# Spectral mixer behind linear attention: pinning filler products in the last four modes, and waiting per PSUM bank instead of per pair of banks

## The chip, the cores and the metric

One core of one Trainium2 chip. The metric is the device time of one execution in microseconds (us). The profiled span, from the first to the last instruction, is about 1.8 us shorter than the timed execution.

## The reference

```python
# linear attention with phi = elu + 1, on q, k, v of shape (8, 8, 576, 64)
q_p, k_p = phi(q), phi(k)
kv  = einsum('bhsd,bhse->...', k_p, v)                  # per head 64 x 64
x   = (q_p @ kv) / (q_p @ sum(k_p) + 1e-6)              # -> (8, 576, 512)
# spectral mix: 64 complex modes, each with its own 512 x 512 complex matrix
X   = rfft(x, axis=1)
Y[:, :64] = X[:, :64] @ (w_r + 1j * w_i)                # mode by mode
u   = x + irfft(Y, n=576)
out = u + relu(u @ w_ch)                                # float32
```

(The first einsum is shortened.) The two weight arrays hold 64 x 512 x 512 float32 each, 134 MB together; everything else is small beside them.

## The kernel before

While the weights stream in, one mode per 4.9 us, TensorE multiplies each mode and computes in the gaps what doesn't depend on the spectrum. What is left for after the last weight is the tail: the last rows of the spectrum through `w_ch`, then 36 output tiles of 128 x 512, taken two at a time ("pairs", 18 of them). A pair owns two banks of PSUM, the memory into which TensorE writes its products; here a bank holds one tile of 128 x 512 float32. Each bank is filled with the channel product of x (`channels`), the inverse transform of the spectrum's channel product is added and rectified in place by ScalarE (`rectified`), then the inverse transform itself is added by TensorE, and VectorE adds x and the tile is stored (`finish`).

```python
def keep_warm(n):                      # filler products, result never read
    for _ in range(n):
        nc.tensor.matmul(last_ps[0], id16, wch16[:, 0, :])

def mode_product(kk, ...):
    for t, w in ((1, wr), (0, wi)):
        ...  nc.tensor.matmul(P..., xt_cols(dc, t, kk), w[...], ...)
        if t == 1 and kk >= NM - 4:
            keep_warm(6)
    ...      # copy P to ys, four matmuls ys -> yt
    if NM - 4 <= kk < NM - 1:
        keep_warm(6)
# [cut]
def channels(n):                       # pair n: one tile, two banks
    accs[n] = pool.tile([128, 2, D], F32, tag="acc", bufs=2, ...)
    for i, t in enumerate(pairs[n]):
        ...  pin(nc.tensor.matmul(accs[n][:, i, cols], id16, src, ...))

def rectified(n):
    for i, t in enumerate(pairs[n]):
        add_inverse(accs[n][:, i], t, 1, ...)
    for i in range(2):
        a = accs[n][:, i]
        pin(nc.scalar.activation(out=a, in_=a, func=AF.Relu))

def finish(n):
    ...      # add_inverse(acc[:, i], t, 0) for both banks, then
    pin(nc.vector.tensor_tensor(out=x, in0=acc, in1=x, op=ALU.add))
    store(t0, 2)                       # the first and the last pair: bank by bank
# [cut]
rectified(0); rectified(1); channels(2); finish(0); channels(3); finish(1)
rectified(2); rectified(3); finish(2)
for n in range(4, len(pairs)):
    channels(n); rectified(n); finish(n - 1)
finish(len(pairs) - 1)
```

`pin` keeps an instruction in program order on its engine; what is not pinned the scheduler may move. Waits between engines follow from which instruction touches which tile, and the two banks of a pair are one tile.

Of the kernel before, what the change touches and what calls it, by code (L numbers as in the profile page):

```python
# [13 lines left out]
AF = mybir.ActivationFunctionType  # L14
ALU = mybir.AluOpType
# [32 lines left out]
def kernel(  # L48
# [10 lines left out]
    nc = tc.nc  # L59

    B, H, S, Dh = q.shape
    D = H * Dh
    NM = moe_w_r.shape[0]
    NHP = H // 2
    NDC = D // 128
    NJJ = 4
# [16 lines left out]
    id16 = const.tile([128, 128], F16, name="id16")  # L83
    fwd_sb = const.tile([128, 5, 2 * NM], F16, name="fwd_sb")
    pick_sb = const.tile([128, 16], F16, name="pick_sb")
    wch16 = const.tile([128, NDC, D], F16, name="wch16")
# [10 lines left out]
    def xt_cols(dc: int, t: int, kk: int):  # L97

        c0 = dc * XDC + t * B * NM + kk
        return xt_c[:, c0 : c0 + 31 * NM + 1 : NM]  # L100
# [27 lines left out]
    pin = tc.keep_in_program_order  # L128
# [196 lines left out]
    def w_get(kk: int):  # L325
        if kk not in w_in:
            w_in[kk] = [w_load(kk, half, wpool, "w", W_KEEP) for half in range(2)]
        return w_in.pop(kk)

    def keep_warm(n: int):  # L330

        for _ in range(n):
            nc.tensor.matmul(last_ps[0], id16, wch16[:, 0, :])

    def mode_product(kk: int, ps, stage, yt_ps):

        wr, wi = w_get(kk)
        st = stage.tile([128, D], F16, tag="ystage", bufs=2, name=f"ys{kk}")

        n_part = 2 if kk == NM - 1 else 1  # L340
        pw = D // n_part
        P = [
            ps.tile([128, D], F32, tag="P", bufs=2, name=f"P{kk}_{i}")[:, 0:pw] for i in range(n_part)
        ]
        for t, w in ((1, wr), (0, wi)):
            for i in range(n_part):
                for dc in range(NDC):
                    nc.tensor.matmul(  # L348
                        P[i][dc * 32 : dc * 32 + 32, :], xt_cols(dc, t, kk),
                        w[:, dc, i * pw : i * pw + pw],  # L350
                        start=(t == 1), stop=(t == 0), tile_position=(0, dc * 32),
                    )
            if t == 1 and kk >= NM - 4:
                keep_warm(6)
        for i in range(n_part):
            dst = st[:, i * pw : i * pw + pw]
            if (kk + i) % 2 == 0:
                nc.vector.tensor_copy(out=dst, in_=P[i])  # L358
            else:
                nc.scalar.copy(out=dst, in_=P[i])  # L360
        for ec in range(NDC):
            nc.tensor.matmul(  # L362
                yt_ps[:, ec, kk % 8, :], st[:, ec * 128 : ec * 128 + 128], pick_sb
            )
        if NM - 4 <= kk < NM - 1:
            keep_warm(6)

    while pending:
        w_next()
# [20 lines left out]
    def mode(kk: int):  # L390
        nonlocal yt_ps
        if kk % 8 == 0:
            yt_ps = psW.tile([128, NDC, 8, 2 * B], F32, tag="yt", bufs=1, name=f"yt{kk // 8}")
        mode_product(kk, psW, ystage, yt_ps)
        if kk == NM - 2:
            nc.vector.tensor_copy(out=YT[:, :, NE : NM - 1, :], in_=yt_ps[:, :, 0 : NL - 1, :])
        elif kk == NM - 1:
            nc.vector.tensor_copy(out=YT[:, :, NM - 1, :], in_=yt_ps[:, :, NL - 1, :])
        elif kk % 8 == 7:
            nc.vector.tensor_copy(out=YT[:, :, kk - 7 : kk + 1, :], in_=yt_ps)  # L400
# [13 lines left out]
    def x_of(t: int):  # L414
        if t < B * NJJ:
            return x_main[t // NJJ][:, t % NJJ, :]
        i = t - B * NJJ
        return x_tail[i // 2][:, i % 2, :]

    def e0_parts(t: int):  # L420

        if t < B * NJJ:
            b, jj = divmod(t, NJJ)
            return [(slice(0, D), E0[b][:, jj * D : jj * D + D])]
        i = t - B * NJJ
        hw = D // 2
        return [(slice(h * hw, h * hw + hw), E0[2 * i + h][:, NJJ * D : QW]) for h in range(2)]
# [4 lines left out]
    last_ps = []  # L432
# [64 lines left out]
    last = sW.tile([128, 2, D], F16, tag="last", bufs=1, name="last")  # L497
    EARLY, LATE, BOTH = 1, 2, 3

    def add_inverse(acc, t: int, half: int, what: int = BOTH):  # L500

        mm = lambda o, l, r: pin(
            nc.tensor.matmul(o, l, r, start=False, stop=True, skip_group_check=True)  # L503
        )
        if t < B * NJJ:
            parts = [(t // NJJ, slice(0, 128), slice(t % NJJ * 128, t % NJJ * 128 + 128))]
        else:
            i = t - B * NJJ
            parts = [(2 * i + h, slice(h * 64, h * 64 + 64), slice(512, 576)) for h in range(2)]
        for b, r, sel in parts:  # L510
            if what == BOTH:
                mm(acc[r, :], inv_sb[:, sel], YZ[b][:, half, :])
                continue
            if what & EARLY:
                mm(acc[r, :], inv_sb[: 2 * NE, sel], YZ[b][: 2 * NE, half, :])
            if what & LATE:
                mm(acc[r, :], inv0_sb[:, sel], last[:, half, :])
# [6 lines left out]
            pairs.insert(len(pairs) - 1, (B * NJJ + 2 * k, B * NJJ + 2 * k + 1))  # L524
    N_PRE = 2
    acc_pools: list = []
    accs: dict[int, object] = {}

    def channels(n: int):
        pool = acc_pools[n % 4 // 2]  # L530
        accs[n] = pool.tile([128, 2, D], F32, tag="acc", bufs=2, name=f"acc{n}")
        for i, t in enumerate(pairs[n]):
            for cols, src in e0_parts(t):
                pin(
                    nc.tensor.matmul(  # L535
                        accs[n][:, i, cols], id16, src, start=(cols.start == 0), stop=False,
                        skip_group_check=True,
                    )
                )

    def rectified(n: int):
        for i, t in enumerate(pairs[n]):
            add_inverse(accs[n][:, i], t, 1, LATE if n < N_PRE else BOTH)
        for i in range(2):
            a = accs[n][:, i]
            pin(nc.scalar.activation(out=a, in_=a, func=AF.Relu))  # L546

    def store(t: int, n_t: int):
        if t < B * NJJ:
            b, jj = divmod(t, NJJ)  # L550
            nc.sync.dma_start(
                out=out[b, 0:512, :].rearrange("(r j) d -> r j d", j=NJJ)[:, jj : jj + n_t, :],
                in_=x_main[b][:, jj : jj + n_t, :],
            )
            return
        i = t - B * NJJ
        for hf in range(2):
            (nc.sync, nc.gpsimd)[hf].dma_start(
                out=out[2 * i + hf : 2 * i + 4 : 2, 512:S, :].rearrange("b r d -> r b d"),
                in_=x_tail[i // 2][hf * 64 : hf * 64 + 64, :, :],  # L560
            )

    def finish(n: int):
        acc = accs.pop(n)
        single = n in (0, len(pairs) - 1)
        t0 = pairs[n][0]
        for i, t in enumerate(pairs[n]):
            if n < N_PRE:
                add_inverse(acc[:, i], t, 0, EARLY)
                add_inverse(acc[:, i], t, 0, LATE)  # L570
            else:
                add_inverse(acc[:, i], t, 0)
            if single:
                x = x_of(t)
                pin(nc.vector.tensor_tensor(out=x, in0=acc[:, i], in1=x, op=ALU.add))  # L575
                store(t, 1)
        if single:
            return
        x = x_main[t0 // NJJ][:, t0 % NJJ : t0 % NJJ + 2, :] if t0 < B * NJJ else x_tail[(t0 - B * NJJ) // 2]
        pin(nc.vector.tensor_tensor(out=x, in0=acc, in1=x, op=ALU.add))  # L580
        store(t0, 2)

    done = 0
# [2 lines left out]
    for kk in range(n_early, NM):  # L586
        mode(kk)
        want = min(len(tiles), (kk - n_early + 1) * len(tiles) // n_spread)
        while done < want:
            channel_product(tiles[done])  # L590
            done += 1
        if kk >= NE - 1:
            while rows_done < min(B, 2 * (kk - NE + 2)):
                form_rows(rows_done)
                rows_done += 1
        if kk == NM - 5:
            psB.release()
            acc_pools.append(
                tc.alloc_tile_pool(name="psT0", bufs=1, space=PSUM, side="right", reuse_waits="tile")
            )  # L600
            for n in range(N_PRE):
                channels(n)
                for i, t in enumerate(pairs[n]):
                    add_inverse(accs[n][:, i], t, 1, EARLY)
            last_ps.append(psW.tile([128, D], F32, tag="zl", bufs=1, name="zl0"))


# [4 lines left out]
    for h in range(2):  # L612
        cols = slice(h * hw, h * hw + hw)
        for ec in range(NDC):
# [3 lines left out]
                    start=(ec == 0), stop=(ec == NDC - 1),  # L618
# [15 lines left out]
    )  # L634

    rectified(0)
    rectified(1)
    channels(2)
    finish(0)
    channels(3)  # L640
    finish(1)
    rectified(2)
    rectified(3)
    finish(2)
# [36 lines left out]
```

## Time and profile before

Median 436.77 us (436.39 to 436.78, 3 runs). What matters:

| part of the span (435.0 us) | from – to, us | what ends last |
|---|---|---|
| stream of weights | to 393.9 | DMA |
| last rows, first two pairs | 393.9 – 403.7 | TensorE at half clock, waits between engines |
| pairs in a steady loop | 403.7 – 425.8 | loop of TensorE and ScalarE, 1.37 us a pair |
| last adds, stores, end | 425.8 – 435.0 | VectorE, stores |

From part 4 of the profile's page of before, the chain of waits by engine:

```profile
DMA 67%; PE 16%; DVE 8%; issue 5%; ACT 2%; POOL 1%; POOLq 0%; DVEq 0%; ACTq 0%
```

From part 2 of the same page: granted TensorE clock in tenths, DMA busy share in tenths, and GB/s, in 40 slices of 10.9 us:

```profile
PEclk9996666675559998657667858586665569966998
DMA  8999999999999999999999999999999999991697
GB/s 149 207 207 209 210 209 209 212 214 219 219 211 213 214 214 213 214 213 214 214 212 214 212 215 213 214 214 213 214 214 213 214 213 214 213 204 34 278 329 265
```

DMA is full until slice 35 (slices are counted from 0). GB/s counts what lands in the core: the weights are float32 in memory and bf16 in the core, so a full DMA shows 213 GB/s here. The clock is low in much of the stream, where DMA sets the pace, and it is down again in slices 35 and 36, just where the stream ends. The view of one source line, the fillers (count; min/median/max ns; first and last start in us):

```profile
L333 PE MATMUL zl<-wch,id x42: 376/379/634, 129.8 to 166.3; 128*128 128x512 f16 x42
```

None of the 42 fillers runs where it was wanted, in the last four modes (377 to 394 us): unpinned, all were moved to 130 to 166 us. The table by stretch of before follows; columns are the stretch, its length, busy us and count of TensorE, its weight loads, VectorE, ScalarE, GpSimd, then granted clock, DMA share and GB/s:

```profile
381.00:386.00 5.00, 1.95 (x16) 0.81 (x16) 0.00 (x0) 0.59 (x1) 0.00 (x0) 0.70 1.06 213
386.00:391.00 5.00, 1.62 (x12) 0.56 (x12) 0.90 (x2) 0.00 (x0) 0.00 (x0) 0.50 1.00 200
...
395.50:397.90 2.40, 2.17 (x12) 1.55 (x12) 0.42 (x2) 0.37 (x1) 0.00 (x0) 0.50 0.00 0
397.90:400.20 2.30, 2.12 (x8) 0.75 (x7) 0.18 (x1) 1.48 (x3) 1.24 (x3) 0.54 0.08 24
400.20:403.70 3.50, 2.65 (x12) 1.04 (x11) 1.38 (x2) 1.34 (x3) 1.66 (x4) 1.00 0.40 134
```

TensorE works 1.6 to 2.0 of 5 us, and the clock goes to 0.50; it is back at 1.00 only after 400.2. Lines of the timeline of before (start, us, engine, line, operation, count, and in brackets the idle time before it with what ended it):

```profile
393.90 0.69 PE L348 MATMUL P<-wi,xt_c 128*32 128x256 bf16 x8 [1.77 <-DMA wi<-in_moe_w_i_dram]
...
395.73 1.89 PE L616 MATMUL zl<-wch,YT 128*128 128x256 f16 x8 [0.32 <-DVE YT L398]
...
398.23 1.87 PE L503 MATMUL acc<-last,inv_sb 128*128 128x512 f16 x4 [0.18 <-DVE last L624]
...
401.22 0.69 DVE L575 TENSOR_TENSOR x_main<-acc,x_main 128x512 f32<-128x512 f32 x1 [3.14 <-PE acc L503]
...
401.97 0.38 PE L503 MATMUL acc<-YZ,inv_sb 112*128 112x512 f16 x1 [0.85 <-DVE x_main L575]
...
403.70 1.02 PE L503 MATMUL acc<-YZ,inv_sb 128*128 128x512 f16 x4
...
417.56 1.17 PE L503 MATMUL acc<-YZ,inv_sb 128*128 128x512 f16 x4
...
418.77 2.52 DVE L580 TENSOR_TENSOR x_main<-acc,x_main 128x1024 f32<-128x1024 f32 x2 [0.22 <-PE acc L503]
...
421.50 2.52 DVE L580 TENSOR_TENSOR x_main<-acc,x_main 128x1024 f32<-128x1024 f32 x2 [0.22 <-PE acc L503]
...
427.69 0.38 PE L503 MATMUL acc<-YZ,inv_sb 128*128 128x512 f16 x1 [0.88 <-DVE x_main L575]
...
428.11 0.69 DVE L575 TENSOR_TENSOR x_main<-acc,x_main 128x512 f32<-128x512 f32 x1 [0.47 <-PE acc L503]
```

Lines 393.9 to 398.2 are the serial end of the spectrum. 401.97 and 427.69 show the price of a pair being one tile: TensorE's product for the second bank waits 0.85 and 0.88 us for VectorE's add of the *first* bank. The adds at 418.77 and 421.50 show the steady loop, two pairs in 2.73 us. The four products at 417.56 take 1.17 us, as every second such group of the loop does. The stores in that time:

```profile
DMA to landing us min/median/max: 2.5/4.6/5.5
```

### The profile page before, as it was taken

How to read it: one execution, taken by the hardware profiler on the slowest of the kernel's cores; microseconds unless marked ns; L12 is line 12 of the kernel's file. 1: busy time of each engine (PE TensorE's matmuls, PEld its weight loads, DVE VectorE, ACT ScalarE, POOL GpSimd, SP SyncE). 2: the span in 40 equal slices, each digit the busy share in tenths (PEclk: the TensorE clock that was granted, in tenths of full speed). 3: DMA queues.
4: the chain of work that ended last, by engine and by line, in shares of the span. 5: the costliest groups of instructions: out<-in, count | busy, mean ns of one | idle time of the engine just before them, and what ended most of it. 6: DMA issues, size and time to landing. Idle time of an engine off the chain costs nothing.

```text
span 435.0 us, 6218 instructions
## 1 busy us (share of the span) xinstructions
PE 291.6 (67%) x2542; PEld 153.5 (35%) x2542; DVE 177.2 (41%) x334; ACT 149.4 (34%) x228; POOL 92.5 (21%) x166
## 2 busy tenths in 40 slices
PE   0358877795039786776775676667587779736992
PEld 0346665562015332222222223222233238413340
DVE  1699998963004242223222323322232222211793
ACT  3687666621002222222222222222222223103681
POOL 4232332122122221222121212122112121102000
PEclk9996666675559998657667858586665569966998
DMA  8999999999999999999999999999999999991697
GB/s 149 207 207 209 210 209 209 212 214 219 219 211 213 214 214 213 214 213 214 214 212 214 212 215 213 214 214 213 214 214 213 214 213 214 213 204 34 278 329 265
DMA packets 35563, 92.38 MB, mean 212 GB/s; under 512 B 3152, under 2 KB 16336, under 8 KB 35536
## 3 DMA queue, kind: packets, MB, share of 16 engines
q0 software_dynamic: 32016, 82.52, 97.5%
q1 hardware_dynamic: 3520, 9.47, 5.8%
q8 instruction: 20, 0.33, 0.3%
q14 instruction: 7, 0.06, 0.0%
HBM read 164.07 MB, written 9.44 MB: 399 GB/s over the span
## 4 chain that ended last, share of the span: by engine, by line
DMA 67%; PE 16%; DVE 8%; issue 5%; ACT 2%; POOL 1%; POOLq 0%; DVEq 0%; ACTq 0%
DMA wr<-in_moe_w_r_dram 34%; DMA wi<-in_moe_w_i_dram 25%; DMA k<-in_k_dram 7%; PE acc L503 4%; PE P L348 3%; DVE x L265 3%; PE eps L462 2%; PE z L485 2%; PE acc L535 2%; PE yp L489 1%; DVE qe L195 1%; DVE q L189 1%; DVE k L189 1%; DVE rd L262 1%; DVE ke L195 1%
## 5 line engine op out<-in xcount | busy, mean ns | idle before, releaser
L114 POOL DMA_DIRECT2D wr<-in_moe_w_r_dram x64 | 34.1, 533 | 136.0 <-PE P L348 112.5
L348 PE MATMUL P<-wi,xt_c 128*32 128x512 bf16 (+1 forms) x260 | 40.7, 525 | 32.0 <-DMA wi<-in_moe_w_i_dram 31.9
L348 PE MATMUL P<-wr,xt_c 128*32 128x512 bf16 (+1 forms) x260 | 42.4, 539 | 27.0 <-DMA wr<-in_moe_w_r_dram 25.7
L470 ACT CAST E<-eps 128x512 f16<-128x512 f32 (+1 forms) x40 | 21.4, 544 | 113.8 <-PE eps L462 113.8
L462 PE MATMUL eps<-wch,xTw 128*128 128x512 f16 x144 | 57.7, 545 | 2.5 <-DVE xTw L459 2.3
L114 POOL DMA_DIRECT2D wi<-in_moe_w_i_dram x64 | 34.1, 534 | 102.9 <-PE P L348 73.9
L447 DVE TENSOR_TENSOR x_main<-nw,rd 128x256 f32<-128x256 f32 x64 | 24.2, 420 | 67.2 <-PE nw L146 67.1
L348 PEld LDWEIGHTS <-xt_c 128*32 128x32 bf16 x520 | 25.8, 161 | 71.7 <-issue 42.4
L358 DVE CAST ys<-P 128x512 f16<-128x512 f32 (+1 forms) x33 | 22.5, 682 | 67.3 <-PE P L348 67.2
L360 ACT CAST ys<-P 128x512 f16<-128x512 f32 (+1 forms) x32 | 18.5, 580 | 78.0 <-PE P L348 77.4
L146 PEld LDWEIGHTS <-qT 64*128 64x128 f16 (+1 forms) x640 | 20.3, 123 | 52.3 <-issue 37.5
L362 PE MATMUL yt<-pick_sb,ys 128*128 128x16 f16 x256 | 16.9, 175 | 32.4 <-DMA pick_sb<-row_pick 21.0
L459 DVE COPY xTw<-xTp 128x512 f16<-128x512 f16 x36 | 15.2, 423 | 46.2 <-PE xTp L457 46.1
L362 PEld LDWEIGHTS <-ys 128*128 128x128 f16 x256 | 12.5, 102 | 46.7 <-issue 23.7
L146 PE MATMUL num<-kv,qT 64*128 64x65 f16 (+1 forms) x320 | 13.1, 218 | 21.2 <-ACT kv L242 17.5
L462 PEld LDWEIGHTS <-xTw 128*128 128x128 f16 x144 | 14.3, 119 | 32.0 <-issue 20.9
L182 ACT ACTIVATE qe<-q 128x1152 f16<-128x1152 f16 x16 | 17.8, 1157 | 22.1 <-DMA q<-in_q_dram 22.1
L211 PE MATMUL qTp<-id,qe 128*128 128x128 f16 x144 | 16.8, 312 | 12.3 <-DVE qe L195 11.9
L454 ACT CAST x16w<-x_main 128x512 f16<-128x512 f32 x32 | 19.9, 621 | 13.3 <-DVE x_main L447 12.8
L546 ACT ACTIVATE acc<-acc 128x512 f32<-128x512 f32 x36 | 20.8, 582 | 6.9 <-PE acc L503 6.0
L503 PE MATMUL acc<-YZ,inv_sb 128*128 128x512 f16 (+2 forms) x80 | 20.5, 381 | 3.3 <-DVE x_main L575 1.7
L265 DVE TENSOR_TENSOR x<-num,rd 128x512 f16<-128x512 f32 x32 | 22.1, 692 | 1.1
(65 smaller groups left out, 382.6 us busy)
## 6 DMA issues: line engine op xcount, KB each, us to landing
wr<-in_moe_w_r_dram POOLq DMA_DIRECT2D x64, 512.0 KB, 18.6
wi<-in_moe_w_i_dram POOLq DMA_DIRECT2D x64, 512.0 KB, 18.7
out_dram<-x_main SPq DMA_DIRECT2D x14, 512.0 KB, 4.6
q<-in_q_dram POOLq DMA_DIRECT2D x8, 576.0 KB, 13.1
k<-in_k_dram POOLq DMA_DIRECT2D x8, 576.0 KB, 14.4
v<-in_v_dram POOLq DMA_DIRECT2D x8, 576.0 KB, 16.5
out_dram<-x_main SPq DMA_DIRECT2D x4, 256.0 KB, 3.7
wch<-in_moe_w_ch_dram POOLq DMA_DIRECT2D x1, 512.0 KB, 20.4
```

What stands on the lines that cost most here:

```text
L114: nc.gpsimd.dma_start(out=w, in_=src[kk].rearrange("(p dc) e -> p dc e", dc=NDC))
L146: mm = nc.tensor.matmul(num[hpo][orow, c0 : c0 + 65], qT[rows, hpp, h2, cols], kv_sb[rows, hpp, h2, :])
L265: nc.vector.tensor_tensor(out=dst.rearrange("p (o c d) -> p o c d", o=2, c=4), in0=nv[:, :, :, 0:64], in1=rden.unsqueeze(3).broadcast_to([ ...
L348: nc.tensor.matmul(P[i][dc * 32 : dc * 32 + 32, :], xt_cols(dc, t, kk), w[:, dc, i * pw : i * pw + pw], start=(t == 1), stop=(t == 0), til ...
L358: nc.vector.tensor_copy(out=dst, in_=P[i])
L362: nc.tensor.matmul(yt_ps[:, ec, kk % 8, :], st[:, ec * 128 : ec * 128 + 128], pick_sb)
L447: nc.vector.tensor_tensor(out=x[orow, o * 256 : o * 256 + 256].rearrange("p (c d) -> p c d", c=4), in0=nv[o][:, :, 0:64], in1=rd_all[b][or ...
L454: nc.scalar.copy(out=x16, in_=x)
L462: nc.tensor.matmul(e_ps, xT[:, c, :], wch16[:, c, :], start=(c == 0), stop=(c == NDC - 1))
L470: nc.scalar.copy(out=dst, in_=e_ps[:, cols])
L503: nc.tensor.matmul(o, l, r, start=False, stop=True, skip_group_check=True)
L546: pin(nc.scalar.activation(out=a, in_=a, func=AF.Relu))
```

## The change

Two independent ideas. First, the fillers and the last four modes are pinned, so that fillers run between the late weights and keep TensorE's clock up. (Twelve a mode as before, but three of them now stand ahead of the `ys` products, to cover the copy.) Second, every instruction on a pair tells which banks it uses, and it is declared independent of instructions on the other bank. The order on each engine in the tail stays the same; only waits go.

```diff
     def keep_warm(n: int):
         for _ in range(n):
-            nc.tensor.matmul(last_ps[0], id16, wch16[:, 0, :])
+            pin(nc.tensor.matmul(last_ps[0], id16, wch16[:, 0, :]))
# [cut: products of modes NM-4 and later are pinned in the same way]
+        if NM - 4 <= kk < NM - 1:
+            keep_warm(3)                 # ahead of the ys products
# [cut]
         if NM - 4 <= kk < NM - 1:
-            keep_warm(6)
+            keep_warm(3)
# [cut]
+    users: dict[int, list] = {}
+    def on_bank(n: int, banks: set, ins):
+        pin(ins)
+        for other, theirs in users.setdefault(n, []):
+            if not banks & theirs:
+                tc.declare_no_dep(ins.ins, other.ins, reason="the other bank of the pair")
+        users[n].append((ins, banks))
# [cut: in channels, add_inverse, rectified and finish pin(...) becomes
#  on_bank(n, {i}, ...); the add over a whole pair is on_bank(n, {0, 1}, ...)]
```

More of the change, by code (lines that the diff above doesn't have):

```diff
@@ L347, in mode_product @@
                 for dc in range(NDC):
-                    nc.tensor.matmul(
+                    mm = nc.tensor.matmul(
                         P[i][dc * 32 : dc * 32 + 32, :], xt_cols(dc, t, kk),
@@ L352, in mode_product @@
                     )
+                    if kk >= NM - 4:
+                        pin(mm)
             if t == 1 and kk >= NM - 4:
                 keep_warm(6)
+        if NM - 4 <= kk < NM - 1:
+            keep_warm(3)
         for i in range(n_part):
@@ L361, in mode_product @@
         for ec in range(NDC):
-            nc.tensor.matmul(
+            mm = nc.tensor.matmul(
                 yt_ps[:, ec, kk % 8, :], st[:, ec * 128 : ec * 128 + 128], pick_sb
             )
+            if kk >= NM - 4:
+                pin(mm)
         if NM - 4 <= kk < NM - 1:
-            keep_warm(6)
+            keep_warm(3)
     while pending:
@@ L498, with add_inverse @@
     EARLY, LATE, BOTH = 1, 2, 3
-    def add_inverse(acc, t: int, half: int, what: int = BOTH):
-        mm = lambda o, l, r: pin(
-            nc.tensor.matmul(o, l, r, start=False, stop=True, skip_group_check=True)
+    def add_inverse(n: int, i: int, t: int, half: int, what: int = BOTH):
+        acc = accs[n][:, i]
+        mm = lambda o, l, r: on_bank(
+            n, {i}, nc.tensor.matmul(o, l, r, start=False, stop=True, skip_group_check=True)
         )
@@ L507, in add_inverse @@
         else:
-            i = t - B * NJJ
-            parts = [(2 * i + h, slice(h * 64, h * 64 + 64), slice(512, 576)) for h in range(2)]
+            p = t - B * NJJ
+            parts = [(2 * p + h, slice(h * 64, h * 64 + 64), slice(512, 576)) for h in range(2)]
         for b, r, sel in parts:
@@ L533, in channels @@
             for cols, src in e0_parts(t):
-                pin(
+                on_bank(
+                    n, {i},
                     nc.tensor.matmul(
@@ L537, in channels @@
                         skip_group_check=True,
-                    )
+                    ),
                 )
@@ L542, in rectified @@
         for i, t in enumerate(pairs[n]):
-            add_inverse(accs[n][:, i], t, 1, LATE if n < N_PRE else BOTH)
+            add_inverse(n, i, t, 1, LATE if n < N_PRE else BOTH)
         for i in range(2):
             a = accs[n][:, i]
-            pin(nc.scalar.activation(out=a, in_=a, func=AF.Relu))
+            on_bank(n, {i}, nc.scalar.activation(out=a, in_=a, func=AF.Relu))
     def store(t: int, n_t: int):
@@ L563, in finish @@
     def finish(n: int):
-        acc = accs.pop(n)
+        acc = accs[n]
         single = n in (0, len(pairs) - 1)
@@ L568, in finish @@
             if n < N_PRE:
-                add_inverse(acc[:, i], t, 0, EARLY)
-                add_inverse(acc[:, i], t, 0, LATE)
+                add_inverse(n, i, t, 0, EARLY)
+                add_inverse(n, i, t, 0, LATE)
             else:
-                add_inverse(acc[:, i], t, 0)
+                add_inverse(n, i, t, 0)
             if single:
                 x = x_of(t)
-                pin(nc.vector.tensor_tensor(out=x, in0=acc[:, i], in1=x, op=ALU.add))
+                on_bank(n, {i}, nc.vector.tensor_tensor(out=x, in0=acc[:, i], in1=x, op=ALU.add))
                 store(t, 1)
@@ L579, in finish @@
         x = x_main[t0 // NJJ][:, t0 % NJJ : t0 % NJJ + 2, :] if t0 < B * NJJ else x_tail[(t0 - B * NJJ) // 2]
-        pin(nc.vector.tensor_tensor(out=x, in0=acc, in1=x, op=ALU.add))
+        on_bank(n, {0, 1}, nc.vector.tensor_tensor(out=x, in0=acc, in1=x, op=ALU.add))
         store(t0, 2)
@@ L603 @@
                 for i, t in enumerate(pairs[n]):
-                    add_inverse(accs[n][:, i], t, 1, EARLY)
+                    add_inverse(n, i, t, 1, EARLY)
             last_ps.append(psW.tile([128, D], F32, tag="zl", bufs=1, name="zl0"))
```

## The prediction

> **What bounds the kernel now.** The chain of waits is 67% DMA: weight loads hold the program until about 394 us of the 435.0 us span, and the page's slices show DMA 8 to 9 tenths busy from slice 1 to 35. Nothing in the diff touches that stream. What can move is the 41 us after the last weight lands (393.9 us in the timeline):
>
> 1. 393.9 to 403.7: last mode, its products, first inverse products. The table by stretch gives a granted TensorE clock of 0.50 from 386 to 397.9, 0.54 to 400.2, then 1.00. Eight zl products take 1.89 us and the first four inverse products 1.87, against about 0.22 us each later at clock 1.00.
> 2. 403.7 to 424: paired accumulators, 2.74 us for two pairs (timeline). With starts 0.216 us apart TensorE needs 1.30 us a pair, ScalarE 1.25, VectorE 1.26: 0.07 us a pair is waiting. Both rectifications wait for both banks' products, and the next products for both rectifications.
> 3. 424 to 435: last pair, store, landing.
>
> **Fillers.** They should keep TensorE busy in the last four modes, but unpinned the scheduler put them elsewhere: the trace has all 42 between 129.8 and 166.3 us. The changed order has 6 + 3 + 3 in each of modes 60 to 62 and 6 in mode 63. A mode arrives every 4.9 us; products plus 12 fillers make about 3.8 us of work, gaps below 1 us. The Trainium skill (TensorE: Matmul & The Clock Gate, "The HAM clock gate") says that busyness in windows of 3.4 us decides between half and full rate; the trace agrees (busy 0.45 from 376, clock 0.5 by 386). I expect 1.00 from 376 to the end. Removing fillers at 130 to 166 is worth nothing: DMA bounds there.
>
> Estimates from these durations: last mode's products −0.2 us; zl, transposes and first inverse products −1.5 to −2 (partly hidden, since the transposed copy and four rectifications, 0.59 each, then follow one another on ScalarE). Six fillers before the last half-mode cost 1.3 us at full clock in a gap of 1.77: free. At half clock (2.6 us) they delay by about 0.8.
>
> **Waits per bank.** Tail order on TensorE is unchanged; each rectification waits for one bank, each bank's last product for one rectification. Start (pairs 0 and 1, waits of 0.85 us behind VectorE): −0.5 to −1. Steady part: 1.37 to 1.30 a pair over 14 pairs, −1.0. End: the second bank no longer waits for VectorE on the first (0.88 us), −0.4.
>
> Sum about −4.2. Against it: stores. One pair is 524 kB, at 1.30 us 403 GB/s; the trace shows 399 to 418 GB/s at DMA share 1.0 from 419 to 427, so stores limit as closely as TensorE. The skill (DMA: Bandwidth & Descriptors, "Where 436 GB/s comes from") gives 435 as the fabric's ceiling. I take off 0.5.
>
> **Prediction: 433.0 us, 431.6 to 434.8 (8 in 10). Faster by over 2%: 3%; within 2%: 96%; slower by over 2%: 1%.**
>
> **Right if** clock 1.00 from 381 to 400; fillers between 376 and 393; last weight still near 394; zl's eight take about 1.0 us; two pairs about 2.6 us; the final second-bank product has no VectorE wait; last VectorE add near 425.
>
> **Wrong if** the clock still drops (gain near 2); fillers delay the last mode; stores back up (landing above 5.5 us, gain near 2.5); or waiting per bank adds waits on TensorE that cost what they save.

## The result, and the profile after

Median 432.92 us (432.52 to 433.71, 4 runs) against 436.77 (436.39 to 437.08, 4 runs): ratio 0.9914, interval 0.9897 to 0.9932: a gain clear of noise, and under 2%. Ratios here are the mean time of one kernel's runs over that of the other's of the same rounds, so not quite the ratio of the medians quoted beside them. A later group of rounds, the same kernel again as a control, gave 0.9930 (below).

The same views of after. The page's slices (10.8 us each now):

```profile
PEclk9996676666559766657658577566555866999997
DMA  8999999999999999999999999999999999993797
GB/s 148 207 208 209 209 209 209 211 213 215 222 211 213 216 212 213 213 213 213 213 214 214 213 213 213 214 214 214 214 214 213 213 213 213 214 213 77 292 330 281
```

The fillers:

```profile
L333 PE MATMUL zl<-wch,id x42: 376/379/390, 379.7 to 393.1; 128*128 128x512 f16 x42
```

The table by stretch, same columns:

```profile
381.00:386.00 5.00, 4.95 (x32) 1.76 (x31) 0.69 (x1) 0.39 (x1) 0.00 (x0) 1.00 1.05 211
386.00:391.00 5.00, 4.73 (x33) 1.79 (x31) 0.94 (x2) 0.20 (x1) 0.00 (x0) 1.00 0.99 198
391.00:395.50 4.50, 3.11 (x28) 1.38 (x26) 0.93 (x3) 0.37 (x1) 0.00 (x0) 1.00 0.26 52
395.50:397.90 2.40, 1.86 (x15) 1.33 (x16) 0.52 (x2) 1.14 (x3) 0.07 (x1) 1.00 0.00 0
397.90:400.20 2.30, 2.30 (x12) 1.05 (x11) 0.96 (x2) 1.87 (x4) 2.30 (x5) 1.00 0.25 71
400.20:403.70 3.50, 3.32 (x16) 1.33 (x15) 2.47 (x3) 2.33 (x5) 0.53 (x2) 1.00 0.71 255
```

TensorE is busy nearly all of the time to 391 us and 3.11 of the next 4.50 us, and the clock stays at 1.00. The weights do not come later: share and rate from 381 to 391 are those of before. Lines of the timeline:

```profile
394.05 0.48 PE L348 MATMUL P<-wi,xt_c 128*32 128x256 bf16 x8 [0.54 <-DMA wi<-in_moe_w_i_dram]
...
395.65 1.05 PE L632 MATMUL zl<-wch,YT 128*128 128x256 f16 x8 [0.32 <-DVE YT L404]
...
397.31 1.02 PE L510 MATMUL acc<-last,inv_sb 128*128 128x512 f16 x4 [0.39 <-DVE last L640]
...
399.24 1.29 DVE L591 TENSOR_TENSOR x_main<-acc,x_main 128x512 f32<-128x512 f32 x2 [2.08 <-PE acc L510]
...
400.78 1.96 PE L510 MATMUL acc<-YZ,inv_sb 128*128 128x512 f16 x6
...
413.82 1.03 PE L510 MATMUL acc<-YZ,inv_sb 128*128 128x512 f16 x4
...
415.12 1.03 PE L510 MATMUL acc<-YZ,inv_sb 128*128 128x512 f16 x4
...
416.42 1.03 PE L510 MATMUL acc<-YZ,inv_sb 128*128 128x512 f16 x4
...
420.53 1.92 PE L510 MATMUL acc<-YZ,inv_sb 128*128 128x512 f16 x8
...
422.93 1.28 DVE L591 TENSOR_TENSOR x_main<-acc,x_main 128x512 f32<-128x512 f32 x2
```

The eight `zl` products take 1.05 us instead of 1.89, the first four inverse products 1.02 instead of 1.87. The third pair's products start at 400.78 instead of 403.70. Each group of four inverse products comes 1.30 us after the last (413.82, 415.12, 416.42), so two pairs take 2.60 us. At 420.53 eight products run without a break: the last second bank no longer waits for VectorE. The last adds end at 422.93 + 1.28 = 424.21 us. The stores:

```profile
DMA to landing us min/median/max: 2.6/4.8/5.9
```

To compare runs whose last weight lands at slightly different times (393.7 to 394.9 us), I count from the start of the last weight product. "Third pair" is the start of its first inverse product, "tail add" the start of the last-but-one pair's add, "last add" the end of the last add; the drain is from there to the end of the span.

| us | before | after | after − before |
|---|---|---|---|
| last weight product → third pair | 9.80 | 6.73 | −3.07 |
| third pair → tail add | 22.12 | 21.01 | −1.11 |
| tail add → last add | 2.98 | 2.42 | −0.56 |
| drain | 6.2 | 6.7 | +0.5 |
| sum | 41.1 | 36.9 | −4.2 |

### The profile page after: what moved, and what is told of

It is laid out like the page before. It is cut to its first block, busy times and chain, and to the rows that moved or that the text cites. A ratio compares the mean times of both kernels' runs of the same rounds, so it can differ in the third digit from the quotient of the medians. Undisturbed runs are those within 1.5% of the kernel's fastest.

```text
span 430.9 us, 6215 instructions
## 1 busy us (share of the span) xinstructions
PE 297.7 (69%) x2542; PEld 154.3 (36%) x2542; DVE 176.9 (41%) x334; ACT 147.3 (34%) x228; POOL 92.3 (21%) x166
## 5 line engine op out<-in xcount | busy, mean ns | idle before, releaser
L468 PE MATMUL eps<-wch,xTw 128*128 128x512 f16 x144 | 61.4, 575 | 3.7 <-DVE xTw L465 3.2
L348 PE MATMUL P<-wr,xt_c 128*32 128x512 bf16 (+1 forms) x260 | 45.6, 560 | 23.5 <-DMA wr<-in_moe_w_r_dram 21.5
L348 PE MATMUL P<-wi,xt_c 128*32 128x512 bf16 (+1 forms) x260 | 44.7, 538 | 23.0 <-DMA wi<-in_moe_w_i_dram 23.0
L348 PEld LDWEIGHTS <-xt_c 128*32 128x32 bf16 x520 | 24.8, 164 | 58.8 <-issue 28.3
L182 ACT ACTIVATE qe<-q 128x1152 f16<-128x1152 f16 x16 | 17.7, 1155 | 22.9 <-DMA q<-in_q_dram 22.9
L463 PE MATMUL xTp<-id,x16w 128*128 128x128 f16 x144 | 19.5, 278 | 4.0 <-ACT x16w L460 4.0
L562 ACT ACTIVATE acc<-acc 128x512 f32<-128x512 f32 x36 | 19.1, 581 | 5.4 <-PE acc L510 3.8
```

The lines of the kernel that those rows point to most:

```text
L348: mm = nc.tensor.matmul(P[i][dc * 32 : dc * 32 + 32, :], xt_cols(dc, t, kk), w[:, dc, i * pw : i * pw + pw], start=(t == 1), stop=(t == 0) ...
L463: nc.tensor.transpose(xT_ps[:, c, :], x16[:, c * 128 : c * 128 + 128], id16)
L468: nc.tensor.matmul(e_ps, xT[:, c, :], wch16[:, c, :], start=(c == 0), stop=(c == NDC - 1))
L562: on_bank(n, {i}, nc.scalar.activation(out=a, in_=a, func=AF.Relu))
```

## The experiments

Theory A: two separate gains, clock and waits, each about half. Its rivals (the clock is off the critical path; each part needs the other; it is the order of the modes) and later ones on the stores stand in the expectations. All edits are small ones of the changed kernel. Here are all results in one table, on the measure of the last section; the runs between two dashes are a group that shared its rounds and its runs of before (the three groups ran on one chip). All are with a correct result but for the three with half the stores, which are wrong:

| run | median, us | ratio (interval) | weight product → last add | drain |
|---|---|---|---|---|
| after, first | 432.92 | 0.9914 (0.9897–0.9932) | 30.16 | 6.7 |
| — | | | | |
| e1_fillers_only | 435.15 | 0.9953 (0.9940–0.9965) | 33.41 | 6.3 |
| e2_banks_only | 435.36 | 0.9954 (0.9942–0.9967) | 32.12 | 7.0 |
| e3_no_fillers | 435.16 | 0.9955 (0.9942–0.9969) | 32.29 | 6.4 |
| e4_half_stores | 432.49 | 0.9889 (0.9875–0.9902) | 30.17 | 6.2 |
| — | | | | |
| c_after_again | 433.78 | 0.9930 (0.9919–0.9942) | 30.16 | 7.2 |
| e5_banks_steady | 435.04 | 0.9959 (0.9947–0.9971) | 32.26 | 6.5 |
| e6_banks_start | 433.89 | 0.9933 (0.9920–0.9946) | 31.89 | 6.2 |
| e8_tail_pair_earlier | 433.58 | 0.9929 (0.9915–0.9942) | 30.20 | 7.8 |
| — | | | | |
| e4b_half_stores | 432.09 | 0.9885 (0.9869–0.9901) | 30.17 | 6.2 |
| e10_start_half_stores | 433.54 | 0.9916 (0.9902–0.9930) | 31.88 | 5.6 |
| e9b_tail_sync | 432.73 | 0.9899 (0.9885–0.9913) | 30.17 | 6.7 |
| e7_third_fillers | 434.96 | 0.9951 (0.9934–0.9968) | 31.59 | 7.1 |

Before took 34.90 us on this measure (428.80 − 393.90), drain 6.2; its medians in the three groups were 437.12, 436.90 and 437.21.

### Each part alone

Fillers alone (the waits as before):

```diff
-            if not banks & theirs:
+            if False:
```

> Only the pinned fillers and the pinned last four modes; the accumulators wait per pair as before. Theory A (two separate gains: the clock is worth about half, the waits the other half): clock 1.00 from 376 to 400 us, zl products about 1.0 us instead of 1.89, first inverse products about 1.0 instead of 1.87, two pairs still 2.74 us; time about 435.0 us (ratio 0.995 to 0.997). Rival B (the clock at the end is off the critical path, the waits give all): time 436.8, ratio within 0.002 of 1. Rival C (each part is worth little without the other): above 436.

Banks alone (`keep_warm` and the modes unpinned and placed as before):

```diff
-            pin(nc.tensor.matmul(last_ps[0], id16, wch16[:, 0, :]))
+            nc.tensor.matmul(last_ps[0], id16, wch16[:, 0, :])
# and no pin on the products of the last four modes; keep_warm(3) + (3) again 6 at the end
```

> Only the waits per bank; fillers and modes unpinned as before. Theory A: clock 0.5 from 386 to about 400, two pairs 2.6 us, last second-bank product without a VectorE wait; time about 434.8 us (gain about 2.0: steady part 1.1, end 0.5, start 0.4). Rival B: 433.0, the whole gain. Rival C: above 436.

No fillers, everything else as changed:

```diff
-        for _ in range(n):
+        for _ in range(0):
```

> The changed kernel with its pinned modes and waits per bank but no filler at all. Theory A: the same as with the waits alone (434.8, within 0.4 of e2), because fillers at 130 to 166 us cost nothing there and the order of the modes is worth nothing; clock 0.5 from 386. Rival D (it is the pinned order of the last modes, not the clock, that helps): near 433.

Measured: 0.9953, 0.9954 and 0.9955. Each part alone gives about 2.0 us, and their sum, 0.93% or 4.1 us, is a little over what both give together (0.86% at first, 0.70% in the control). So rivals B and C are out. Taking the fillers away altogether equals leaving them where the scheduler had put them, although the modes stay pinned: fillers at 130 to 166 us cost nothing, and the order of the modes alone buys nothing (no run has one without the other, so that the two cancel is not excluded). Rival D, that the order gives the gain, is out. The table by stretch of the kernel without fillers shows the clock falling as in before:

```profile
381.00:386.00 5.00, 1.42 (x12) 0.56 (x12) 0.00 (x0) 0.58 (x1) 0.00 (x0) 0.74 1.08 216
386.00:391.00 5.00, 1.63 (x12) 0.56 (x12) 0.79 (x2) 0.00 (x0) 0.00 (x0) 0.50 0.99 198
```

### How many fillers the clock needs

```diff
-        for _ in range(n):
+        for _ in range(n // 3):
```

> The changed kernel with a third of the fillers (14 instead of 42: 2 + 1 + 1 a mode, 2 in the last). TensorE then works about 2.2 of every 4.9 us. Theory A (the clock is what the fillers buy, and half a stretch of work does not hold it): clock falls to 0.5 before 391, as without fillers; ratio 0.995. Rival U (short gaps suffice whatever the share of work): clock 1.00 to 400 and ratio 0.993.

Measured: ratio 0.9951, as with none. The stretches 381 to 386, 386 to 391 and 395.5 to 397.9 of its table:

```profile
381.00:386.00 5.00, 2.37 (x19) 0.95 (x20) 0.12 (x1) 0.59 (x1) 0.00 (x0) 1.00 1.07 215
386.00:391.00 5.00, 3.46 (x16) 0.80 (x16) 0.62 (x1) 0.00 (x0) 0.00 (x0) 0.50 0.98 196
...
395.50:397.90 2.40, 2.00 (x12) 1.39 (x13) 0.47 (x2) 0.37 (x1) 0.00 (x0) 0.50 0.00 0
```

2.37 busy us of 5 lost the clock (the 3.46 in the next stretch are 16 products at half speed), so rival U is out for gaps of this length. The longest wait of TensorE in the first stretch of the timeline was 1.43 us. With all fillers it works 3.11 of 4.50 us (391 to 395.5) in the least busy of these stretches and keeps the clock. So in these last modes a limit on the share, if that is what counts, lies between about half and 70%. It is not a rule for the whole kernel, though. Earlier in before the clock fell after a stretch that was busy 2.73 of 3.40 us, with many small products:

```profile
96.20:99.60 3.40, 2.73 (x35) 1.83 (x35) 3.23 (x9) 0.00 (x0) 1.06 (x2) 1.00 1.06 213
99.60:103.00 3.40, 2.61 (x16) 1.49 (x16) 1.39 (x3) 0.39 (x1) 0.53 (x1) 0.51 1.07 214
```

No run here settles what exactly counts as work.

### Which of the waits matter

Waits per bank only for pairs 2 to 16 (the steady loop), and only for pairs 0 and 1:

```diff
-            if not banks & theirs:
+            if not banks & theirs and 2 <= n < len(pairs) - 1:   # e5
+            if not banks & theirs and n < 2:                     # e6
```

The control and the two:

> The changed kernel unaltered, as the control of this group: ratio 0.991 to 0.992 as at first; 3.26 us from the last weight product to the first inverse product, 30.2 us from there to the end of the last VectorE add counted from the last weight product, drain 6.5 to 6.8 us.

> Pinned fillers, and waits per bank only for the pairs from the third to the last but one; the first two and the last pair wait as before. From the fillers-only run (33.4 us from last weight product to last add) theory A takes 1.1 for the steady part: 32.3 us, two pairs 2.59 us, last pair as in before (VectorE wait of about 0.9 us before the second bank); time about 1 us under fillers-only, ratio 0.993. Rival F (the steady part is paced by stores or by VectorE, the gain is all start and end): 33.2 us or more, ratio 0.995.

> Pinned fillers, and waits per bank only for the first two pairs. Theory A: the third pair's rectification products start about 1.6 us earlier than with fillers only, two pairs stay at 2.74 us, last pair as before; 31.8 us from last weight product to last add, ratio 0.992. Rival G (what the start gains is lost again while the steady loop catches up): third pair early, but 33 us to the last add and ratio 0.995.

On the engines both did to the tenth what theory A said: against the 33.41 us of the fillers alone, the steady part takes 1.15 us (32.26), the start 1.52 (31.89). The start's gain is two waits of TensorE that the kernel with fillers alone still has; in after the same two products, at 398.60 and 399.04, follow without a wait:

```profile
399.23 0.38 PE L510 MATMUL acc<-YZ,inv_sb 112*128 112x512 f16 x1 [0.42 <-ACT acc L562]
...
400.68 0.38 PE L510 MATMUL acc<-YZ,inv_sb 112*128 112x512 f16 x1 [0.85 <-DVE x_main L591]
```

In time the two did not do as expected: e5 came to 0.9959, no better than the fillers alone in the other group, and e6 to 0.9933, the same as the whole change (0.9930). The control itself missed its expectation (0.9930, not 0.991 to 0.992; drain 7.2). The start of the tail pays in part: e6 is 0.20%, 0.9 us, under the fillers alone of the other group, of 1.52 us on the engines. The 1.7 us by which the whole change makes the last add earlier than e6 (30.16 against 31.89) show up in time as 0.1 us. The two profiles taken give a larger part: 37.4 − 38.1 = −0.7 us from weight product to the end of the span. In them the last weight product of e6 started 0.4 us earlier (394.11 against 394.52 us), which hides as much in time: the end of the stream varies by itself, and enters every time.

### Where those 1.7 us go: the stores

Half of the x_main bytes not stored, but for the first and the last pair (the outputs are wrong: unwritten rows):

```diff
-        store(t0, 2)
+        store(t0, 1 if t0 < B * NJJ else 2)
```

> The changed kernel with only the first row group of each x_main pair stored (wrong result on purpose): about half the bytes of the tail. Theory A (TensorE paces the tail, stores only lengthen the drain): two pairs stay at 2.59 us, last VectorE add stays near 424.2 us, the drain after it shrinks from 6.7 to about 5.7 us, time about 432. Rival E (stores pace the tail): two pairs below 2.5 us, last VectorE add before 423, time below 430.5.

> The half-stores kernel once more (wrong result on purpose), as the partner of the next run: ratio 0.989, last VectorE add 30.2 us after the last weight product, drain near 6.2.

The same on top of e6:

> Waits per bank for the first two pairs alone, and half the stores (wrong result on purpose). With all stores this change of waits made no difference in time (0.9933 against 0.9930) although the last add came 1.7 us later. Theory S (the stores' stream sets the end, so TensorE's gain of the steady part and the end is swallowed): with half the stores the 1.7 us come back, ratio 0.9925 to 0.993 against 0.989 of the partner, drain equal in both. Rival T (the 1.7 us are lost to something else): within 0.5 us of the partner.

With half the stores the last add stays at 30.17 us after the last weight product: stores do not pace TensorE (rival E is out). The time falls to 0.9889 and 0.9885. And now the waits of the steady part and the end are worth 433.54 − 432.09 = 1.45 us, where they were worth 0.11 with all stores; the runs of the two kernels do not overlap (433.32 to 433.93 against 431.81 to 432.49), while with all stores they do (433.58 to 434.54 against 433.17 to 434.28). That is what theory S expects, that the stores swallow it; rival T is out. The table by stretch, 417 to 423 us, of after and of the half-stores kernel shows the difference in DMA share, last column but one (a share a little over 1 is to be read as full):

```profile
417.00:419.00 2.00, 2.00 (x13) 0.98 (x10) 1.86 (x3) 1.78 (x4) 0.00 (x0) 1.00 1.03 412
419.00:421.00 2.00, 2.00 (x12) 0.65 (x10) 1.70 (x2) 1.32 (x4) 0.00 (x0) 1.00 1.03 404
421.00:423.00 2.00, 1.38 (x7) 0.25 (x6) 1.73 (x3) 1.02 (x2) 0.00 (x0) 1.00 1.01 406
```

```profile
417.00:419.00 2.00, 2.00 (x15) 0.93 (x13) 1.86 (x3) 1.60 (x4) 0.00 (x0) 1.00 0.56 202
419.00:421.00 2.00, 2.00 (x14) 0.65 (x10) 1.70 (x2) 1.50 (x3) 0.00 (x0) 1.00 0.63 237
421.00:423.00 2.00, 1.00 (x6) 0.11 (x2) 1.74 (x3) 0.64 (x2) 0.06 (x1) 1.00 0.44 163
```

The case isn't closed, though. The size of the effect (1.45 − 0.11 = 1.3 us) is about as large as its uncertainty, as I reckon it from the four intervals (1.2 us). These hold the scatter of before as well; from the single runs of the four kernels alone it is 1.3 us with a standard error of 0.3. But the single profiles show less of it: e10 against e4b differs by 1.1 us from weight product to end, the control against e6 by 0.7. The absolute 0.9925 to 0.993 that I expected of e10 was also too high (0.9916), and its drain was not equal to the partner's (5.6 against 6.2).

Two more tries on the stores:

```diff
-            pairs.insert(len(pairs) - 1, (B * NJJ + 2 * k, ...))          # e8
+            pairs.insert(len(pairs) - 1 if k == 0 else 9, (B * NJJ + 2 * k, ...))
-            (nc.sync, nc.gpsimd)[hf].dma_start(                            # e9b
+            (nc.sync, nc.sync)[hf].dma_start(
```

> The changed kernel with the second pair of row tails moved from the last but one place to the tenth. Its stores use the DMA engines badly (share 1.0 at 240 to 290 GB/s). Theory A (end paced by TensorE, drain by backlog): last add within 0.3 us of the control, drain 6.2 instead of 6.7 us, ratio 0.990. Rival H (the total of bytes sets the end, whatever the order): same as the control within 0.001.

Measured: 0.9929 against the control's 0.9930, with the last add in place and the drain longer (7.8), not shorter. Moving the inefficient stores changes nothing; rival H.

> The changed kernel with both halves of each row-tail store on SyncE's queue instead of one on GpSimd's, whose packets of 4096 bytes took 241 ns on the mean against 163 on the other queue. Theory S: stores set the end, so cheaper packets shorten it by 0.3 to 0.8 us: ratio 0.9905 to 0.9925. Rival: no difference from the changed kernel (0.993).

Measured: 0.9899, below what I expected, and the best ratio of any variant with a correct result; the median of 432.73 us is under both of the changed kernel's. But it did not run in one group with that kernel, whose own ratio moved from 0.9914 to 0.9930 between groups, and its profile (drain 6.7 us) shows no gain over after's 6.7. The packet records speak against the reason that I gave, too. The two halves of a row-tail store are alike, 262 kB each. In the first one of after, SyncE's half went in 128 packets of 2048 bytes that took 20.3 us of DMA-engine time together, GpSimd's in 64 packets of 4096 bytes that took 17.7. With both halves on SyncE they took 37.0 us instead of 38.0, which is 0.06 us over 16 engines. So a gain of 0.7 to 1.4 us is possible, not shown, and cheaper packets would not explain it.

## Why the prediction was right

The time, 433.0 predicted and 432.92 measured, agrees better than its terms do; that it came within 0.1 us is luck.

- **Fillers: right in mechanism and size.** Predicted clock 1.00 from 376 to the end (measured 1.00 in every stretch to 424), `zl` about 1.0 us (1.05), last weight near 394 (394.05), −1.7 to −2.2 us in all. Alone they gave 0.47%, 2.0 us in time; on the engines it was a little less, 1.48 us from the last weight product to the third pair (9.80 to 8.32). The claim that fillers at 130 to 166 us cost nothing fits the kernel without fillers, with the reserve made there.
- **Start of the waits: mechanism right, size too small.** Predicted −0.5 to −1 us for pairs 0 and 1. With the clock already up, the third pair starts 1.6 us earlier (8.32 us after the last weight product with the fillers alone, 6.73 with both). The prediction counted the wait behind VectorE (0.85) and left out the one behind ScalarE (0.42).
- **Steady part: right on the engines** (−1.0 predicted, −1.1 measured; 1.30 us a pair), **and end** (−0.4 predicted, −0.56 measured).
- **Stores: right that they are the second limit, too small.** I took off 0.5 us. The profile of after has exactly that, a drain of 6.7 instead of 6.2 us, and the control has 7.2. The timed runs say more: of the 1.7 us of the steady part and the end almost nothing is paid out, and halving the stores gives back 0.25 to 0.45% (1.1 to 2.0 us, compared across groups). The longest landing rose from 5.5 to 5.9 us, past the limit in the warning of the prediction; the gain did not fall to the 2.5 us named there.

So terms were mis-sized in opposite directions and cancelled: the start was too small by about 0.85 us against the middle of its range; the fillers on the engines were too large by about 0.5, and the stores too small by 0.4 to 1.1 us (the last add is 4.74 us earlier, the medians 3.85 and 3.12 us, so 0.9 to 1.6 us were lost where I took off 0.5). My reading of it is that a step in the compute chain pays for the most part as long as the store stream has slack, which is at the start of the tail, and hardly once DMA is full; the experiments support this but, as said, do not settle how much is swallowed.

The skill was of use in two places. TensorE: Matmul & The Clock Gate, "The HAM clock gate", says that a window of 3.4 us of activity switches between full and half rate: the stretches show 1.00 and 0.50 with mixtures where a stretch holds both, and the four products at 398.23 in before are still slow. The traces' clock records agree with the length: the clock was at half for 17.07 us in before (from 382.96) and for 13.65 us with a third of the fillers (from 385.96), five and four times 3.41. DMA: Bandwidth & Descriptors, "Where 436 GB/s comes from", gives 435 GB/s as the fabric's ceiling: the tail's stores reach 404 to 412 GB/s in the stretches above at a DMA share of 1.03.

## What to carry to other kernels

A filler that nothing reads is free to the scheduler: look in the trace where it runs before crediting it, and pin it where the clock is needed. Waits between banks of one tile can be dropped at no cost in work, but ask for each stage what ends last there. As far as these runs show, a gain ahead of a full store stream starts that stream earlier and counts; the same gain while the stream is full mostly lengthens the queue.

## What the Trainium skill lacked or had wrong

- TensorE: Matmul & The Clock Gate, "Why this matters for your kernels", advises no idle gaps over about 3 us. That is not enough: the clock went to 0.50 in before with waits of at most 2.00 us between products (busy 1.95 of 5 us), and with a third of the fillers with waits of at most 1.43 us (busy 2.37 of 5). It held at 3.11 of 4.5 (after, 391 to 395.5). No share is given on the page beyond its remark that micro-idles make the clock oscillate; and one share would not fit all of before, where the clock also fell after 2.73 busy us of 3.40.
- DMA: Bandwidth & Descriptors, "Where 436 GB/s comes from", says that for transfers between HBM and SBUF the HBM side, about 358 GB/s, binds. The stores of this one core ran at 404 to 412 GB/s over 2 us stretches; for one core alone the 435 is the nearer figure. The same page's measured table has that for loads (425 GB/s, the pair's other core idle); it has none for stores.
- DMA: Bandwidth & Descriptors, "Issuing engine by pattern", calls the queues of SyncE generally faster than GpSimd's without a figure for stores. In DMA-engine time no advantage shows here: of two equal halves of a row-tail store in after, SyncE's took 20.3 us and GpSimd's 17.7. The means that the expectation of e9b compares, 241 and 163 ns for packets of 4096 bytes, belong to stores of different shape.
